# Attention and a SwiGLU block in one kernel: the block's tokens cut into twelve tiles of 512, 512 and 128 instead of nine of 512

## The chip, the core and the metric

The kernel runs on one core of one Trainium2 chip. The metric is the device time of one execution in microseconds (us); of several runs the median is given. A core has five engines with instruction streams of their own: TensorE (PE), VectorE (DVE), ScalarE (ACT), GpSimd (POOL) and SyncE (SP), which here only issues transfers. Each stream is executed in order, and the streams meet at semaphores.

## What is computed

Attention with a forget gate on 8 batches of 8 heads, 576 tokens and 64 columns a head; then the heads' outputs side by side are the 4608 x 512 input of a gated feed-forward block (FFN) with 1536 inner columns.

```python
def _attn_ref(q, k, v, f):
    B, H, S, D = q.shape
    scores = 1.0 / np.sqrt(D) * np.matmul(q, k.transpose(0, 1, 3, 2))
    cum = np.cumsum(np.log(np.clip(f, 0.0001, 1.0)), axis=-1)
    decay = cum[:, :, :, None] - cum[:, :, None, :]
    causal = np.triu(np.ones((S, S), dtype=bool), k=1)
    scores = np.where(causal, -1000000000.0, scores + decay)
    attn = np.exp(scores - np.max(scores, axis=-1, keepdims=True))
    attn = attn / (np.sum(attn, axis=-1, keepdims=True) + 1e-09)
    return np.matmul(attn, v)

def reference(q, k, v, f, moe_w_gate, moe_w_val, moe_w_out):
    x = _attn_ref(q, k, v, f).transpose(0, 2, 1, 3).reshape(4608, 512)
    g = x @ moe_w_gate
    return (g * (1.0 / (1.0 + np.exp(-g))) * (x @ moe_w_val)) @ moe_w_out
```

## The kernel before

**Order.** The program is not written in the order in which it runs. Each piece of work is an `Op` with the engines that may run it, an estimated duration, what it comes after, the buffers it takes and a key. `Plan.run` plays the pieces forward in an estimated time: whenever an engine is free, it takes the ready piece with the lowest key whose buffers are free, and emits its instructions. What comes out is a fixed order on each engine. `ORDER` overrides the keys of the earliest pieces with tuned numbers. `release(p)` gives the estimated time at which a pair of heads may start to load (PACE0, PACE_A and PACE are its offset and its steps; LEAD is how much earlier the conversion of Q and K to bf16 in DRAM is issued on POOL).

**Attention.** Two heads are a pair, four pairs a batch. Scores (`score`, L703) have keys on the partitions and come in four banks of PSUM a head: 7 matmuls, 1600 columns. ACT takes the exponential (`expo`, L737), POOL zeroes the triangle on the diagonal (`mask`, L746), PE weighs the values (`weigh`, L760, 15 matmuls of 65 columns a head, the last column being the sum), DVE inverts the sum and scales (`invert` L767, `scale` L772). The result is transposed into `xT`, a ring for the inputs of six batches (6 x 576 = 3456 columns).

**FFN.** Tokens go in tiles t = 0 to 8 of 512, each cut into 12 chunks (fc) of 128 inner columns. `gate` (L918) makes one chunk's gate or value in one PSUM bank: 4 matmuls of 512 columns, or 8 where a tile wraps round the ring. `tanh` (ACT, L922) and `silu` (DVE, L932) form the activation, `times` (DVE, L935) multiplies it by the value into `HH`. From chunk ALONE on, when all exponentials are done, ACT computes the whole activation with another table (`whole`, L925) and `silu` falls away.

The projection by `w_out` (`wo`) comes in two forms. Tiles t < QUICK use `simple`: 48 matmuls of 512 columns (`project`, L976), copies on ACT (L979), four stores. The others use `finish`, one level of a seven-product scheme in the manner of Strassen over blocks of tokens, inner columns and outputs: `sums` (DVE, L960) prepares three operands for each pair of chunks (512, 512 and 256 columns), `product` (L969) does 2 x 42 matmuls of 256 columns, and ACT (L985), POOL (`both` L992, `apart` L1017) and DVE (`more` L996, `close` L1020) combine the pieces in `OT`. The weights that this needs are made from `wo` by `blend` (DVE, L948 and L950), ten operations of which the last four overwrite `wo` itself, so they come after the last plain projection. The last tile has a finer ending of its own (L1001 to L1013), with stores from SP and ACT.

**Buffers.** PSUM has eight banks: pool f with four (gates and values, also products), s with two (scores), o and t with one each. After the planner's time WIDE_AT the FFN may use all eight. V comes through NNV buffers `natv` by SP's queue (`ld_v`, L612) and is converted on POOL. The transposes of Q and K (`turned`, L599), the gate rows (L602), the transposes of the outputs (`cross`, L790) and most stores also go through SP's queue.

Of the kernel before, what the change touches and what calls it, by code (L numbers as in the profile page):

```python
# [10 lines left out]
BF16 = mybir.dt.bfloat16  # L11
AF = mybir.ActivationFunctionType
ALU = mybir.AluOpType
# [21 lines left out]
class Plan:  # L35
# [163 lines left out]
HALF = 256  # L199
RING = 6  # L200
# [7 lines left out]
OFFS = [0, 0, 576, 1024]  # L208
PT_W = 1408
PADS = (512, 960, 1344)  # L210
NQK, NPT0, NPT, NVB, NNV, NXN, NTH, NHH, NSU, NOT, NRC = 8, 6, 5, 3, 5, 4, 4, 7, 6, 2, 4
FIRST = 2
CROSS = (8, 9, 10)
PACE = 8.6
LATE = 2.5
PACE_A = 9.0
PACE0 = 59.0
LEAD = 14.0


@with_exitstack
def kernel(ctx, tc, q, k, v, f, w_gate, w_val, w_out, out):
    nc = tc.nc
    B, H, S, D = q.shape
    BH = B * H
    N_TOK, DM = out.shape
    DFF = w_gate.shape[1]
    P = 128
# [3 lines left out]
    KD = DM // P  # L232
    KF = DFF // P
    MT = 512
# [5 lines left out]
    FCG, FCO = KF // NCG, KF // NCO  # L240
# [27 lines left out]
    TH = [sb(f"th{i}", [P, MT], F32) for i in range(NTH)]  # L268
    HH = [sb(f"hh{i}", [P, 2, MT], BF16) for i in range(NHH)]
    SU = [sb(f"su{i}", [P, 5, HALF], BF16) for i in range(NSU)]  # L270
    OT = [sb(f"ot{i}", [P, 2, DM], F32) for i in range(NOT)]
    wt = sb("wt", [P, 3, KF // 2, HALF], BF16)
    ident = sb("ident", [P, P], BF16)
# [7 lines left out]
    def ps(b):  # L281
        return bank[bank_of[b.pool] + b.i]
# [12 lines left out]
    QN = [[t.rearrange("p (u x) -> p u x", u=2) for t in ts] for ts in (  # L295
        [SU[r].rearrange("p n c -> p (n c)")[:, : 2 * S] for r in range(KD)], [xT[:, r, 4 * S : 6 * S] for r in range(KD)])]

    plan = Plan(
        {"f": 4, "s": 2, "o": 1, "t": 1, "qk": NQK, "pt0": NPT0, "pt": NPT, "vb": NVB, "nv": NNV,
         "xn": NXN, "rc": NRC, "th": NTH, "hh": NHH, "su": NSU, "ot": NOT},  # L300
        lambda t: 2.0 if t < TWARM else 1.0,
    )
# [165 lines left out]
    def blank(e, what):  # L468
# [46 lines left out]
        else:  # L515
            if what != "rest":
                fill32(e, VB[what][:, :, :, D:].bitcast(F32), ONE2)
            if what:
# [4 lines left out]
              after=[op(("DVE", 0.07), lambda e: nc.vector.memset(warm, 1.0), key=-30)])  # L523
# [23 lines left out]
    for h, name, i in fixed + [(hqk[FB + p], "qk", 2 + p) for p in range(FB)]:  # L547
        h.pool, h.i = name, i
        plan.free[name].remove(i)
    release = lambda p: 0.0 if p < 2 * FB else PACE0 + min(p - 2 * FB, FB) * PACE_A + max(p - 3 * FB, 0) * PACE  # L550

# [240 lines left out]
    x_ready, crossed = {}, {}  # L792
# [30 lines left out]
    exps = []  # L823
# [87 lines left out]
    def gate(e, w, fc, t0, n, bf):  # L911
        lo = t0 % (RING * S)
        cut = min(n, RING * S - lo)
        for ko in range(KD):
            for a, b in ((0, cut), (cut, n)):
                if a < b:
                    at = (lo + a) % (RING * S)
                    nc.tensor.matmul(ps(bf)[:, a:b], w[:, ko, fc * P : (fc + 1) * P], xT[:, ko, at : at + b - a],  # L918
                                     start=ko == 0 and a == 0, stop=ko == KD - 1 and b == n)

    def tanh(e, n, bf, bt):
        nc.scalar.activation(TH[bt.i][:, :n], ps(bf)[:, :n], AF.Tanh, scale=0.5)  # L922

# [10 lines left out]
    def times(e, n, bf, bt, bh, r, lo, by):  # L934
        nc.vector.scalar_tensor_tensor(out=HH[bh.i][:, r, lo : lo + n], in0=TH[bt.i][:, :n], scalar=by, in1=ps(bf)[:, :n],  # L935
                                       op0=ALU.mult, op1=ALU.mult)

    wq = wo.rearrange("p (g e) (s d) -> p e s g d", e=2, s=2)
    B11, B12, B21, B22 = [wq[:, i, j] for i in range(2) for j in range(2)]
    T1, T6, T7 = [wt[:, i] for i in range(3)]  # L940
    T3, T4 = B12, B21
# [10 lines left out]
    def sums(e, n, bh, bu):  # L952
        h, u = HH[bh.i], SU[bu.i]
        if n == 0:
# [17 lines left out]
    def project(e, hs, q, a, bf, gs):  # L972
        lo = a * HALF + q * P
        for g in gs:
            for r in range(2):
                nc.tensor.matmul(ps(bf), HH[hs[g].i][:, r, lo : lo + P], wo[:, 2 * g + r], start=g + r == 0, stop=2 * g + r == KF - 1)  # L976

    def out_copy(e, a, bf, bo):
        nc.scalar.activation(OT[bo.i][:, a], ps(bf), AF.Copy)  # L979

    def store2(e, t0, bo):
        E[e].dma_start(out=bass.AP(out.tensor, out.offset + t0 * DM, [[DM, P], [HALF * DM, 2], [1, DM]]), in_=OT[bo.i])

    def mid_copy(e, bf, bo):
        nc.scalar.activation(OT[bo.i].rearrange("p a d -> p (a d)")[:, HALF : 3 * HALF], ps(bf), AF.Copy)  # L985

    def edges(bo):
        return OT[bo.i].rearrange("p a (s d) -> p (a s) d", s=2)[:, 0::3]

# [35 lines left out]
    w_ready = {}  # L1025
    last_gate = [None]
    tails = []

    before, tabled = [], []

    def unit(t, fc, t0, n, hs, lo, kk, after):
        if (t, fc) == ALONE:
            tabled.append(op(("ACT", 1.4), turn_table, after=before + exps, key=-6, tag="table"))
# [9 lines left out]
        if fresh:  # L1043
            hs[p].gate = g
        alone = (t, fc) >= ALONE
        if alone:
# [13 lines left out]
    read = []  # L1060

    def ffn(t, t0, n):
        key, hs, ms = 1e5 * (t + 1), [None] * (KF // 2), []
        for fc in range(KF):
            parts = [(0, HALF), (HALF, n - HALF)] if t == 0 and fc < WIDE else [(0, n)]
            ms.append([])
            for u, (lo, w) in enumerate(parts):
                lg, m = unit(t, fc, t0 + lo, w, hs, lo, key + 100 * fc + 50 * u, [last_gate[0]])
                ms[fc].append(m)
        last_gate[0] = lg  # L1070
        tails.append((t, t0, key, hs, ms))

    plain = []

# [105 lines left out]
            queries(p, 1000 * b + 100 * (p % FB) + 10)  # L1180
    for p in range(FB, BH // 2):
        attention(p, 1000 * (p // FB) + 1000 + 100 * (p % FB))
    for t, t0 in enumerate(range(0, N_TOK, MT)):
        ffn(t, t0, MT)
    for r in tails[:QUICK]:
        simple(*r)
    ready = [w_ready["o", c] for c in range(NCO)]
    blended = [op({e: f((KF // 2) * HALF // 2) + 0.35 * (n // 2 == 1) for e, f in BLEND_ON.items()}, blend, n, after=ready, key=BLEND_KEY + n, ready=BLEND_AT, tag=("blend", n)) for n in range(6)]
    blended += [op({e: f((KF // 2) * HALF // 2) for e, f in BLEND_ON.items()}, blend, n, after=blended[:6] + plain, key=BLEND_KEY + n, ready=BLEND_AT, tag=("blend", n)) for n in range(6, 10)]
    for r in tails[QUICK:]:  # L1190
        finish(*r, blended)

    for a, b, done in x_ready.values():
        for lo, hi, ops in read:
# [13 lines left out]

QUICK = 3


def F_POOLS(t):
    return ("f",) + tuple((x, WIDE_AT, 1e9) for x in "sot")
# [6 lines left out]
def fast(n):  # L1222
    return (n / 2 + 110) / 960
# [11 lines left out]
BOTH_ON = {"POOL": pool2}  # L1235
APART_ON = {"POOL": pool2}
BLEND_ON = {"DVE": fast}
BLEND_AT = 150.0
POOL_KEY = 50000
ALONE = (6, 6)  # L1240
LAST_ON = {"DVE": slow}
VB1_KEY = 2
QKZ_KEY = -26
# [124 lines left out]
```

## Time and profile before

| | |
|---|---|
| median of 3 runs | 378.27 us (378.03 to 378.41) |
| the profiled execution | 378.08 us |
| its span, first to last instruction | 376.4 us |
| PE busy | 368.8 us, 3427 matmuls |
| DVE busy | 249.4 us, 575 instructions |
| ACT busy | 214.4 us |
| POOL busy | 161.4 us |
| granted PE clock | 1.0 |

Lines of the profile name an engine, the line of the kernel (L918), the tile written and those read, the shape, the count, the busy time and the mean of one in ns, then the idle time of the engine before them and what ended it. "PEld" is the loading of PE's stationary operand, which overlaps PE. A "window" is the busy time of each engine in a stretch of the span. The "chain" follows the work that ended last back through what released it.

### The profile page before, as it was taken

How to read it: one execution, taken by the hardware profiler on the slowest of the kernel's cores; microseconds unless marked ns; L12 is line 12 of the kernel's file. 1: busy time of each engine (PE TensorE's matmuls, PEld its weight loads, DVE VectorE, ACT ScalarE, POOL GpSimd, SP SyncE). 2: the span in 40 equal slices, each digit the busy share in tenths (PEclk: the TensorE clock that was granted, in tenths of full speed). 3: DMA queues.
4: the chain of work that ended last, by engine and by line, in shares of the span. 5: the costliest groups of instructions: out<-in, count | busy, mean ns of one | idle time of the engine just before them, and what ended most of it. 6: DMA issues, size and time to landing. Idle time of an engine off the chain costs nothing.

```text
span 376.4 us, 9092 instructions
## 1 busy us (share of the span) xinstructions
PE 368.8 (98%) x3427; PEld 233.6 (62%) x3427; DVE 249.4 (66%) x575; ACT 214.4 (57%) x438; POOL 161.4 (43%) x388
## 2 busy tenths in 40 slices
PE   8999999999999999999999999999999999999996
PEld 5667655455565555555685558655887776467465
DVE  7979886277526674499737994598638844753664
ACT  7999962265656754746576467555774433333332
POOL 8897546033633643465376437732462013003000
PEclk9999999999999999999999999999999999999999
DMA  8999998859988998999699999995325003002003
GB/s 145 192 198 195 206 204 151 185 100 180 174 187 169 166 189 160 228 191 180 117 160 200 228 149 143 243 206 99 72 74 93 2 2 111 2 0 81 33 0 114
DMA packets 125163, 52.01 MB, mean 138 GB/s; under 512 B 111823, under 2 KB 119695, under 8 KB 124351
## 3 DMA queue, kind: packets, MB, share of 16 engines
q1 hardware_dynamic: 108478, 35.95, 49.2%
q0 software_dynamic: 16288, 15.14, 26.9%
q8 instruction: 27, 0.44, 0.5%
q10 hardware_dynamic: 352, 0.34, 0.3%
q14 instruction: 18, 0.14, 0.1%
HBM read 38.56 MB, written 17.07 MB: 148 GB/s over the span
## 4 chain that ended last, share of the span: by engine, by line
PE 94%; DMA 2%; DVE 1%; POOL 1%; ACT 1%; issue 1%; DVEq 0%; POOLq 0%
PE ps L918 49%; PE ps L969 14%; PE ps L703 10%; PE ps L976 8%; PE ps L760 8%; DMA su<-in_k_dram 2%; PE ps L721 1%; PE ps L777 1%; PE ps L578 1%; POOL su L554 1%; PE ps L729 0%; PE ps L1201 0%; ACT PT L737 0%; DVE hh L935 0%; DVE xn L772 0%
## 5 line engine op out<-in xcount | busy, mean ns | idle before, releaser
L918 PE MATMUL ps<-xT,wv 128*128 128x512 bf16 (+2 forms) x496 | 111.7, 351 | 0.0
L918 PE MATMUL ps<-xT,wg 128*128 128x512 bf16 (+2 forms) x496 | 111.5, 351 | 0.0
L737 ACT ACTIVATE PT<-ps 128x384 bf16<-128x384 f32 (+2 forms) x192 | 91.6, 510 | 14.8 <-PE ps L703 9.7
L935 DVE SCALAR_TENSOR_TENSOR hh<-th,ps 128x512 bf16<-128x512 f32 (+1 forms) x112 | 74.5, 667 | 21.1 <-PE ps L918 12.9
L922 ACT ACTIVATE th<-ps 128x512 f32<-128x512 f32 (+1 forms) x82 | 47.2, 577 | 54.1 <-PE ps L918 51.8
L746 POOL TENSOR_SCALAR_AFFINE_SELECT PT<-PT 128x128 bf16<-128x128 bf16 (+1 forms) x192 | 54.1, 288 | 44.1 <-ACT PT L737 38.5
L918 PEld LDWEIGHTS <-wg 128*128 128x128 bf16 x496 | 45.1, 97 | 37.9
L918 PEld LDWEIGHTS <-wv 128*128 128x128 bf16 x496 | 45.0, 97 | 38.1
L932 DVE SCALAR_TENSOR_TENSOR th<-th,ps 128x512 f32<-128x512 f32 (+1 forms) x82 | 53.7, 656 | 19.7 <-ACT th L922 19.6
L703 PE MATMUL ps<-QK 68*128 68x256 bf16 x392 | 63.9, 261 | 0.4 <-ACT PTa L737 0.4
L746 POOL TENSOR_SCALAR_AFFINE_SELECT PTa<-PTa 128x256 bf16<-128x256 bf16 x64 | 26.3, 413 | 80.3 <-ACT PTa L737 79.5
L760 PE MATMUL ps<-VB,PT 128*128 128x65 bf16 x768 | 42.0, 193 | 0.0
L703 PEld LDWEIGHTS <-QK 68*128 68x128 bf16 x392 | 31.5, 97 | 14.0 <-issue 0.6
L760 PEld LDWEIGHTS <-PT 128*128 128x128 bf16 x768 | 34.2, 97 | 9.3 <-POOL PT L746 0.9
L737 ACT ACTIVATE PTa<-ps 128x384 bf16<-128x384 f32 x64 | 30.9, 488 | 15.4 <-PE ps L703 14.8
L767 DVE RECIPROCAL rc<-ps 128x5 f32<-128x5 f32 (+2 forms) x68 | 12.8, 188 | 39.6 <-PE ps L760 39.3
L969 PEld LDWEIGHTS <-su 128*128 128x128 bf16 x360 | 34.8, 97 | 4.6
L960 DVE TENSOR_TENSOR su<-hh 128x512 bf16<-128x512 bf16 (+1 forms) x108 | 36.7, 384 | 0.9
L925 ACT ACTIVATE th<-ps 128x512 f32<-128x512 f32 x30 | 17.9, 596 | 32.1 <-PE ps L918 32.1
L976 PE MATMUL ps<-wo,hh 128*128 128x512 bf16 x144 | 34.8, 379 | 0.0
L772 DVE TENSOR_TENSOR xn<-ps,rc 128x320 bf16<-128x320 f32 (+2 forms) x72 | 32.4, 454 | 2.2
L969 PE MATMUL ps<-wt,su 128*128 128x256 bf16 x216 | 29.0, 272 | 0.0
(97 smaller groups left out, 323.1 us busy)
## 6 DMA issues: line engine op xcount, KB each, us to landing
out_dram<-ot SPq DMA_DIRECT2D x32, 256.0 KB
natv<-in_v_dram SPq DMA_DIRECT2D x25, 256.0 KB
qk_d<-in_q_dram POOLq DMA_DIRECT2D x24, 144.0 KB, 3.6
qk_d<-in_k_dram POOLq DMA_DIRECT2D x24, 144.0 KB, 4.3
wv<-in_moe_w_val_dram POOLq DMA_DIRECT2D x3, 512.0 KB, 10.6
wg<-in_moe_w_gate_dram POOLq DMA_DIRECT2D x3, 512.0 KB, 12.4
wo<-in_moe_w_out_dram POOLq DMA_DIRECT2D x4, 384.0 KB, 14.1
VB<-in_v_dram POOLq DMA_DIRECT2D x7, 128.0 KB, 8.9
```

The costliest lines, as they stand in the source:

```text
L703: nc.tensor.matmul(s[:, c : c + w], QK[:KR, hqk[p].i, 1, j * S + kt * P : j * S + (kt + 1) * P], QK[:KR, hqk[p].i, 0, j * S + q0 : j * S + ...
L737: nc.scalar.activation(place(h, i)[:, OFFS[i] : OFFS[i] + c], ps(bs)[:, :c], AF.Exp, scale=0.125)
L746: nc.gpsimd.affine_select(out=d, in_=d, pattern=pat, compare_op=ALU.is_ge, fill=0.0, base=0, channel_multiplier=-1,)
L760: nc.tensor.matmul(o[:, lo : lo + D + 1], pt[:, c : c + P], VB[hvb[b].i][:, kt, hb, : D + 1], start=first and n == 0, stop=last and n == l ...
L772: nc.vector.tensor_mul(XN[bx.i][:, qb : qb + nq, j], o, r)
L918: nc.tensor.matmul(ps(bf)[:, a:b], w[:, ko, fc * P : (fc + 1) * P], xT[:, ko, at : at + b - a], start=ko == 0 and a == 0, stop=ko == KD - ...
L922: nc.scalar.activation(TH[bt.i][:, :n], ps(bf)[:, :n], AF.Tanh, scale=0.5)
L932: nc.vector.scalar_tensor_tensor(out=t, in0=t, scalar=1.0, in1=ps(bf)[:, :n], op0=ALU.add, op1=ALU.mult)
L935: nc.vector.scalar_tensor_tensor(out=HH[bh.i][:, r, lo : lo + n], in0=TH[bt.i][:, :n], scalar=by, in1=ps(bf)[:, :n], op0=ALU.mult, op1=ALU ...
L960: E[e].tensor_tensor(out=o, in0=x, in1=y, op=f)
L969: nc.tensor.matmul(ps(bf)[:, c * HALF : (c + 1) * HALF], left(g)[:, q * P : (q + 1) * P], right[:, g], start=opens and g == 0, stop=g == K ...
L976: nc.tensor.matmul(ps(bf), HH[hs[g].i][:, r, lo : lo + P], wo[:, 2 * g + r], start=g + r == 0, stop=2 * g + r == KF - 1)
```

## The change

The tokens are cut into tiles of 512, 512 and 128, four times, so that three tiles are two batches of 576 and no tile wraps round the ring. Tiles of 512 are treated as before, but only tile 0 has the plain projection (QUICK 3 to 1); the other seven have the seven products, so the blends are made earlier (BLEND_AT 150 to 69).

A tile of 128 has functions of its own. `gate4` puts four chunks side by side into one bank, with 16 matmuls of 128 columns; so ACT and DVE still handle 512 columns at a time. `times4` writes the product for four chunks into `NH`, and `pairs` adds neighbouring chunks. `single` projects with H1 B11 + H2 B21 = (H1 + H2) B11 + H2 (B21 - B11), and the same way for the other half of the outputs, since the plain blocks are overwritten by then: 24 matmuls of 256 columns, and in the last tile 12 of 256 and 24 of 128, with three copies and three stores. `lone` orders this.

`natv` goes from 5 to 3 buffers, the loads of the pairs begin somewhat earlier (PACE0, LEAD) with a slightly longer step (PACE), and the activation table is changed at tile 8, chunk 0 instead of tile 6, chunk 6: the same 1280 tokens before the end.

```diff
-NQK, NPT0, NPT, NVB, NNV, NXN, NTH, NHH, NSU, NOT, NRC = 8, 6, 5, 3, 5, 4, 4, 7, 6, 2, 4
+NQK, NPT0, NPT, NVB, NNV, NXN, NTH, NHH, NSU, NOT, NRC = 8, 6, 5, 3, 3, 4, 4, 7, 6, 2, 4
-PACE = 8.6
+PACE = 8.7
-PACE0 = 59.0
-LEAD = 14.0
+PACE0 = 57.0
+LEAD = 16.0
...
+    NH = sb("nh", [P, 3 * KF // 2, P], BF16)
...
+    def gate4(e, w, fq, t0, bf):
+        lo = t0 % (RING * S)
+        for c in range(4):
+            for ko in range(KD):
+                nc.tensor.matmul(ps(bf)[:, c * P : (c + 1) * P], w[:, ko, (4 * fq + c) * P : (4 * fq + c + 1) * P], xT[:, ko, lo : lo + P],
+                                 start=c + ko == 0, stop=c == 3 and ko == KD - 1)
...
+    def times4(e, fq, bf, bt, by):
+        nc.vector.scalar_tensor_tensor(out=NH[:, 4 * fq : 4 * fq + 4].rearrange("p a c -> p (a c)"), in0=TH[bt.i], scalar=by, in1=ps(bf),
+                                       op0=ALU.mult, op1=ALU.mult)
+
+    def pairs(e, fq):
+        h = NH[:, 4 * fq : 4 * fq + 4].rearrange("p (g e) c -> p e g c", e=2)
+        E[e].tensor_tensor(out=NH[:, KF + 2 * fq : KF + 2 * fq + 2], in0=h[:, 0], in1=h[:, 1], op=ALU.add)
...
+    def single(e, s, gs, bf, c0, c1, opens, closes):
+        lo = s * HALF
+        for g in gs:
+            for n, (left, right) in enumerate(((KF + g, B11), (2 * g + 1, T4)) if s == 0 else ((2 * g, T3), (KF + g, B22))):
+                nc.tensor.matmul(ps(bf)[:, c0:c1], NH[:, left], right[:, g, c0 - lo : c1 - lo],
+                                 start=opens and g + n == 0, stop=closes and g + n == KF // 2, skip_group_check=True)
+
+    def part_copy(e, bf, bo, c0, c1):
+        copy(e, OT[bo.i][:, 0, c0:c1], ps(bf)[:, c0:c1])
...
+    def ffn1(t, t0):
+        key, bn, ms, first = 1e5 * (t + 1), Buf("nh"), [], []
+        for fq in range(KF // 4):
...
+            g = op(("PE", mm(*[P] * 4 * KD)), gate4, wg, fq, t0, bg, after=needs + wr + [last_gate[0]], behind=first, take=[bg] + ([] if fq else [bn]), key=kk, tag=("gp", t, 4 * fq))
...
+                b = op(("DVE", dve(MT)), silu, MT, bg, bt, after=[b], use=[bg, bt], key=-5, tag=("silu", t, 4 * fq))
+            a = op(("PE", mm(*[P] * 4 * KD)), gate4, wv, fq, t0, bv, after=[g], take=[bv], key=kk + 1, tag=("vp", t, 4 * fq))
+            m = op(("DVE", dve(MT)), times4, fq, bv, bt, 1.0 if alone else 0.5, after=[a, b] + first, use=[bv, bt, bn], key=-5, tag=("mul", t, 4 * fq))
+            ms.append(op({"DVE": fast(HALF)}, pairs, fq, after=[m], use=[bn], key=-5, tag=("pairs", t, fq)))
...
+    def lone(t, t0, key, bn, ms, blended):
+        bo, end, taken = Buf("ot"), t0 + P == N_TOK, False
+        cuts, last, bf = ((0, HALF), (HALF, HALF + P), (HALF + P, DM)) if end else ((0, HALF), (HALF, DM)), [], None
+        for n, (c0, c1) in enumerate(cuts):
...
+            for fq in range(KF // 4):
+                gs = (2 * fq, 2 * fq + 1)
+                last = [op(("PE", mm(*[c1 - c0] * 4)), single, c0 // HALF, gs, bf, c0, c1, opens, closes, after=blended + [ms[fq]] + last,
+                           take=[bf] if opens and not fq else [], use=[bn] + ([] if opens and not fq else [bf]), key=key + 2000 + 100 * n + fq + (150, 51, 0)[n] * (end and fq > 1), tag=("fo", t, n, fq))]
+            if closes:
...
+                c = op(("DVE", dve(c1 - lo)) if end and n else ("ACT", act(c1 - lo)), part_copy, bf, bo, lo, c1, after=last, take=[] if n and end else [bo], use=[bf] + ([bo] if n and end else []),
+                       key=-4, tag=("ot", t, n))
+                op(("ACT" if end and n == 1 else "SP", 0.45 if end else 0.7), store, t0, 0, bo, slice(lo, c1), after=[c], use=[bo], key=-4, dma=0.5 if end else 1.0, packet=90, tag=("out", t, n))
...
-    for t, t0 in enumerate(range(0, N_TOK, MT)):
-        ffn(t, t0, MT)
+    t0 = 0
+    for t, n in enumerate(TILES):
+        ffn(t, t0, n) if n == MT else ffn1(t, t0)
+        t0 += n
...
-        finish(*r, blended)
+        (finish if TILES[r[0]] == MT else lone)(*r, blended)
...
-QUICK = 3
+QUICK = 1
+TILES = (512, 512, 128) * 3 + (512, 512, 128)
...
-BLEND_AT = 150.0
+BLEND_AT = 69.0
-ALONE = (6, 6)
+ALONE = (8, 0)
```

More of the change, by code (lines that the diff above doesn't have):

```diff
@@ L299 @@
         {"f": 4, "s": 2, "o": 1, "t": 1, "qk": NQK, "pt0": NPT0, "pt": NPT, "vb": NVB, "nv": NNV,
-         "xn": NXN, "rc": NRC, "th": NTH, "hh": NHH, "su": NSU, "ot": NOT},
+         "xn": NXN, "rc": NRC, "th": NTH, "hh": NHH, "nh": 1, "su": NSU, "ot": NOT},
         lambda t: 2.0 if t < TWARM else 1.0,
@@ L1071, in ffn @@
         tails.append((t, t0, key, hs, ms))
+    def ffn1(t, t0):
+        key, bn, ms, first = 1e5 * (t + 1), Buf("nh"), [], []
+        for fq in range(KF // 4):
+            if (t, 4 * fq) == ALONE:
+                tabled.append(op(("ACT", 1.4), turn_table, after=before + exps, key=-6, tag="table"))
+            needs = [o for a, b, done in x_ready.values() if a < t0 + P and b > t0 for o in done]
+            wr = [w_ready[n, c] for n in "gv" for c in range(4 * fq // FCG, (4 * fq + 3) // FCG + 1)]
+            bg, bv, bt = Buf(*F_POOLS(t)), Buf(*F_POOLS(t)), Buf("th")
+            kk = key + 400 * fq
+            g = op(("PE", mm(*[P] * 4 * KD)), gate4, wg, fq, t0, bg, after=needs + wr + [last_gate[0]], behind=first, take=[bg] + ([] if fq else [bn]), key=kk, tag=("gp", t, 4 * fq))
+            first = first or [g]
+            alone = (t, 4 * fq) >= ALONE
+            if alone:
+                b = op(("ACT", act(MT)), whole, MT, bg, bt, after=[g] + tabled, take=[bt], use=[bg], key=-5, tag=("tanh", t, 4 * fq))
+            else:
+                b = op(("ACT", act(MT)), tanh, MT, bg, bt, after=[g], take=[bt], use=[bg], key=-5, tag=("tanh", t, 4 * fq))
+                before.append(b)
+                b = op(("DVE", dve(MT)), silu, MT, bg, bt, after=[b], use=[bg, bt], key=-5, tag=("silu", t, 4 * fq))
+            a = op(("PE", mm(*[P] * 4 * KD)), gate4, wv, fq, t0, bv, after=[g], take=[bv], key=kk + 1, tag=("vp", t, 4 * fq))
+            m = op(("DVE", dve(MT)), times4, fq, bv, bt, 1.0 if alone else 0.5, after=[a, b] + first, use=[bv, bt, bn], key=-5, tag=("mul", t, 4 * fq))
+            ms.append(op({"DVE": fast(HALF)}, pairs, fq, after=[m], use=[bn], key=-5, tag=("pairs", t, fq)))
+            read.append((t0, t0 + P, [g, a]))
+        last_gate[0] = g
+        tails.append((t, t0, key, bn, ms))
@@ new lines, in lone @@
+    def lone(t, t0, key, bn, ms, blended):
+        bo, end, taken = Buf("ot"), t0 + P == N_TOK, False
+        cuts, last, bf = ((0, HALF), (HALF, HALF + P), (HALF + P, DM)) if end else ((0, HALF), (HALF, DM)), [], None
+        for n, (c0, c1) in enumerate(cuts):
+            opens = bf is None or end
+            if opens:
+                bf, last = Buf(*F_POOLS(t)), []
+            closes = end or c1 == DM
+            for fq in range(KF // 4):
[3 more added lines that the diff above has]
+            if closes:
+                lo = c0 if end else 0
+                c = op(("DVE", dve(c1 - lo)) if end and n else ("ACT", act(c1 - lo)), part_copy, bf, bo, lo, c1, after=last, take=[] if n and end else [bo], use=[bf] + ([bo] if n and end else []),
+                       key=-4, tag=("ot", t, n))
+                op(("ACT" if end and n == 1 else "SP", 0.45 if end else 0.7), store, t0, 0, bo, slice(lo, c1), after=[c], use=[bo], key=-4, dma=0.5 if end else 1.0, packet=90, tag=("out", t, n))
```

## The prediction, made before the changed kernel ran

> **What bounds the kernel now.** I read the page's busy table and slices first, then the windows of 20 us, then who waits on PE, and last the chain in order of time with the groups by shape.
>
> ```profile
> span 376.4 us, 9092 instructions
> ...
> PE 368.8 (98%) x3427; PEld 233.6 (62%) x3427; DVE 249.4 (66%) x575; ACT 214.4 (57%) x438; POOL 161.4 (43%) x388
> ...
> PE   8999999999999999999999999999999999999996
> ```
>
> PE is busy in every slice but the first and the last, so the time is PE's stream of matmuls, plus its gaps, plus what follows the last matmul. Small gaps do not show in that digit, since a matmul's modelled end overlaps the next one. The chain gives the spacing:
>
> ```profile
> 66.08 0.46 PE ps L760 x15
> ...
> 286.25 19.19 PE ps L918 x168
> 305.44 9.17 PE ps L969 x84
> 314.61 20.72 PE ps L918 x96
> ```
>
> 84 products of 256 columns in 9.17 us are 109.2 ns each; 96 gate matmuls of 512 columns in 20.72 us are 215.8 ns each. The difference is 106.6 ns for 256 columns, 0.4164 ns a column, which leaves 2.6 ns for each matmul whatever its width. The 168 are 8 of 512 and 80 pairs of 384 and 128 (the tile that wraps round the ring): (19.19 - 1.73)/80 = 218.3 ns a pair, 2.5 ns more than one of 512. So a split costs the fixed part and nothing else. The second engine is DVE:
>
> ```profile
> 60.00:80.00 20.00, 20.00 (x147) 10.43 (x146) 8.69 (x19) 5.83 (x11) 3.79 (x9) 1.00 0.93 172
> ...
> 160.00:180.00 20.00, 19.44 (x147) 10.26 (x146) 19.06 (x40) 10.81 (x23) 11.51 (x25) 1.00 1.09 182
> 180.00:200.00 20.00, 19.49 (x219) 15.32 (x217) 10.40 (x27) 14.01 (x31) 12.56 (x31) 1.00 0.90 159
> 200.00:220.00 20.00, 19.87 (x143) 10.35 (x141) 18.40 (x38) 10.36 (x22) 8.57 (x21) 1.00 1.08 187
> ```
>
> (The stretch, PE, PEld, DVE, ACT and POOL busy.) From 160 to 180 us, the gates of the first tile with seven products, DVE has 19.06 of 20 us, and just there and after it PE loses 0.56, 0.51 and 0.13 us. The page's waits of PE name it:
>
> ```profile
> PE ps L1201 <- DVE warm L523: 1.1, 1, 1.1
> PE ps L760 <- DVE xn L772: 0.6, 1, 0.6
> PE ps L562 <- DMA su<-in_k_dram: 0.5, 2, 0.4
> ```
>
> The first and the third are the start; no later wait of PE in that view names a DMA.
>
> **The change part by part.** Counts are of the two programs in their order; durations from the rows.
>
> *Matmuls.* Up to tile one's first two gates (about 75 us) PE's order is the same. After that, two tiles' plain projections go: 3 x 48 matmuls of 512 become 48. Products of 256 go from 504 to 588 (seven tiles instead of six), the four narrow tiles project with 108 matmuls in 24576 columns, and their gates are 384 matmuls of 128. Tiles and batches now fit the ring, so the 96 splits of the wrapped tile vanish. In all 861760 columns become 858688, and 3427 matmuls become 3715. That is -3072 x 0.4164 = -1.28 us and +288 x 2.6 ns = +0.75 us: **-0.53 us**. No row of before has a long run of 128-column gate matmuls, each with its own weight load; I bound the fixed part by 2.5 ns (the split pairs) below, and above by the load not hiding, which is a rival below. I take 2.6, because a 65-column matmul with a full load of its own comes every 0.46/15 = 31 ns, well under the 56 ns of a 128-column one.
>
> The Trainium skill's page "TensorE: Matmul & The Clock Gate", section "Back-to-back issue gap", says that in a real stream of load and multiply pairs a matmul of 128 columns takes about 81 ns instead of 56. By it the 384 narrow gates would cost some 9.6 us more (an estimate from that page) and the change would lose. The same passage gives 131 ns for 512 columns, where this trace has 215.8; the trace decides.
>
> *DVE.* Per group:
>
> ```profile
> L935 DVE SCALAR_TENSOR_TENSOR hh<-th,ps 128x512 bf16<-128x512 f32 x104 | 71.3, 686 | 20.7 <-PE ps L918 12.9 <-PE ps L703 0.6
> L932 DVE SCALAR_TENSOR_TENSOR th<-th,ps 128x512 f32<-128x512 f32 x74 | 50.4, 681 | 18.8 <-ACT th L922 18.8
> L960 DVE TENSOR_TENSOR su<-hh 128x512 bf16<-128x512 bf16 x72 | 28.4, 427 | 0.9
> L772 DVE TENSOR_TENSOR xn<-ps,rc 128x320 bf16<-128x320 f32 x56 | 27.5, 491 | 1.8
> L960 DVE TENSOR_TENSOR su<-hh 128x256 bf16<-128x256 bf16 x36 | 10.8, 299 | 0.0
> L767 DVE RECIPROCAL rc<-ps 128x5 f32<-128x5 f32 x56 | 10.7, 191 | 38.0 <-PE ps L760 37.8
> L1020 DVE TENSOR_TENSOR ot<-ps,ot 128x512 f32<-128x512 f32 x11 | 7.6, 690 | 16.0 <-POOL ot L1017 14.9 <-PE ps L703 0.9
> L996 DVE TENSOR_TENSOR ot<-ps,ot 128x256 f32<-128x256 f32 x12 | 5.1, 425 | 13.4 <-POOL ot L992 5.3 <-PE ps L969 4.1 <-POOL PTa L746 2.1
> ...
> L948 DVE TENSOR_TENSOR wt<-wo 128x768 bf16<-128x768 bf16 x6 | 3.1, 551 | 0.0
> ...
> L948 DVE TENSOR_TENSOR wo<-wo 128x768 bf16<-128x768 bf16 x4 | 2.5, 662 | 0.0
> ```
>
> One more tile with sums adds 12 x 0.427 + 6 x 0.299 = 6.9 us, its closing 2 x (0.425 + 0.690) = 2.2, the twelve `pairs` at 0.299 (same size as the narrow sum) 3.6: 12.7 us, DVE 249 to 262. The average is harmless; what counts is DVE against PE between a tile's first and last value gate. Before, tile 3 has 12 `times`, 11 `silu`, 9 wide and 4 narrow sums, 6 blends (2 and 4) and 5 heads' norms (0.682 each): 27.9 us, against 88 gates, 28 scores and 75 weighings on PE, 24.0 us: 3.9 too much. Tile 4: 24.9 against 23.5, 1.4 too much. What that cost shows from the first gate to the first product:
>
> ```profile
> 155.29 1.03 PE L918 MATMUL ps<-xT,wg 128*128 128x512 bf16 x4
> ...
> 183.63 0.82 PE L969 MATMUL ps<-wo,hh 128*128 128x256 bf16 x6
> ...
> 198.41 0.81 PE L918 MATMUL ps<-xT,wg 128*128 128x512 bf16 x3
> ...
> 225.34 0.82 PE L969 MATMUL ps<-wo,hh 128*128 128x256 bf16 x6
> ```
>
> Tile 3 took 28.34 us for 213 matmuls with 62737 columns, 26.68 us at the spacing above: 1.66 lost. Tile 4: 26.93 for 26.20, 0.73 lost. About half of the excess each time; the four banks of pool f take up the rest. After the change the blends go into tile 1 (BLEND_AT 69: four stand before its first `silu`, six among its gates). Tile 1: 28.0 against 24.9, 3.1 too much; tile 3: 24.2 against 23.9; tile 4: 24.9 against 24.0; tile 6: 24.9 against 24.3. Half of these: 1.5 + 0.15 + 0.45 + 0.3 = 2.4, against 1.66 + 0.73 + nothing for tile 5 (25.6 against 25.8) = 2.4 before. With the blends that still stand in front of tile 1 nothing is sure here: from -1.7 (tile 1's backlog swallowed by the slack that the 8.69 of 20 us at 60 to 80 shows) to +1.6 (all of its 3.1 lost). I take **-0.1**, since the first four blends, 2.2 us, fall into that slack.
>
> *The end.*
>
> ```profile
> 371.84 0.82 PE L969 MATMUL ps<-wt,su 128*128 128x256 bf16 x6
> ...
> 372.46 0.42 DVE L1009 SCALAR_TENSOR_TENSOR ot<-ps,ot 128x256 f32<-128x256 f32 x1
> 372.99 0.42 DVE L1013 TENSOR_TENSOR ot<-ps,ot 128x256 f32<-128x256 f32 x1
> ```
>
> PE ends at 372.66, the last closing at 373.41 behind another closing on DVE, and the span 2.95 us later with the store. After, the last thing is a copy of 128 columns: 0.425 - (0.690 - 0.425)/2 = 0.29 us, with nothing queued ahead of it: 0.1 + 0.29 + 2.95 = 3.35 instead of 3.70. In front of it, the last narrow group needs `times4` (0.69), `pairs` (0.30) and two handovers of some 0.15, 1.3 us, while PE has 8 narrow matmuls of 256 and 8 of 128 columns, 1.32 us. On DVE these also queue behind tile ten's last closing, which waits for POOL:
>
> ```profile
> L985 ACT ACTIVATE ot<-ps 128x512 f32<-128x512 f32 x22 | 13.1, 597 | 20.1 <-PE ps L969 19.9
> L1017 POOL TENSOR_TENSOR ot<-ot 128x512 f32<-128x512 f32 x10 | 12.7, 1266 | 11.3 <-ACT ot L985 11.3
> ```
>
> 0.60 + 1.27 + 0.69 and three handovers are some 3 us after that tile's m2, and PE has 0.66 us of products and 3.6 us of narrow gates there; it just fits. I charge 0.1: **-0.25 us**, bounds -0.4 and +0.3.
>
> *Costed at nothing.* Three natv buffers instead of five: SP's V loads now wait for POOL's casts, and the transposes of Q and K queue behind them on SP. The cover is the lead, which grows by 2 us, and that PE waited for no DMA after the start; without it, each wait on a late transpose reaches the next scores. PACE, PACE0 and LEAD move loads by at most 2 us at both ends. The table load moves with ALONE to the same 1280 tokens from the end. POOL's 4 us more of `both` and `apart` lie in stages in which it has 8.6 to 12.6 of 20 us. Stores go out under the next tile's gates.
>
> Sum: -0.53 - 0.1 - 0.25 = -0.9 us of span. The profiled execution took 378.08 us with its 376.4 of span; less 0.9 is 377.2. The median is 0.19 above that execution, so **377.3 us** is what I compare with 378.27.
>
> **Rivals.**
> - *A tie.* The backlog costs as much more as the end saves, or a late transpose eats 0.5 us: -0.53 + 0.1 or so, 377.8. For it: all three terms are small.
> - *DVE becomes the bound in the gates.* Place: tiles 1, 3, 4 and 6, all with sums now and all during attention; before, only two of its tiles were over. Price: if each loses what tile 3 lost, 4 x 1.66 = 6.6 instead of 2.4, so +4.2 - 0.8 = +3.4: 381.7. It decides once DVE's work passes PE's by more than some 2 us in a gate stage, where the banks no longer take it up; tile 1 passes it, the others by count do not. With only tile 1 at its full 3.1 (+1.6) the time is 379.1.
> - *The narrow weight loads do not hide.* The load of a gate tile lasts 97 ns by its row; if it set the spacing, 384 x (97 - 56) = 15.7 us more, 393. It decides once a load takes longer than the matmul before it and cannot start earlier. Against it stand the 31 ns. (The rule weighed above, of "TensorE: Matmul & The Clock Gate" in the Trainium skill, is this one.)
>
> ```profile
> L918 PEld LDWEIGHTS <-wg 128*128 128x128 bf16 x496 | 45.1, 97 | 37.9
> ```
>
> - *The backlog goes away* with the blends out of the busy stage: -1.7 instead of -0.1, 378.27 - 0.53 - 1.7 - 0.25 = 375.8.
> - *That it does not do what it says* can be left out: the order has 588 products and 384 narrow gates.
>
> **How the numbers follow.** Forecast 0.53 (376.5 to 377.6), tie 0.20, DVE 0.19, narrow loads 0.02, backlog gone 0.06. What a measurement here tells from no change is about 0.2%, 0.76 us, so faster means under 377.5. The forecast's own range reaches to that line, so a little of it is in the tie: faster 0.57, same 0.22, slower 0.21. The range reaches from the backlog's gain, 375.8, to a tile 1 that loses everything and a little of the others, 379.6.
>
> **What would show it.** Runs of sixteen narrow gates taking 0.89 us in the chain (1.3 would be the loads); products 84 in 9.17 as before. Tile 1's gates to its first product: 27.85 us of matmuls; up to 29.5 is the forecast, 31 the DVE rival. No loss at 160 to 220 us beyond half a microsecond. From the last matmul to the end 3.3 to 3.4 us. I would be wrong by a wait of PE on a DMA or on `pairs`, or by tiles 3, 4 and 6 losing over 0.7 us each.

## The result, and the profile after

| | before | after |
|---|---|---|
| median of 7 runs each | 378.31 us (378.03 to 378.84) | 379.36 us (379.29 to 380.35) |
| ratio after / before | | 1.0035, 95% interval 1.0024 to 1.0047 |
| the profiled execution | 378.08 us | 379.88 us |

The changed kernel is slower by 0.35%; 377.3 us was forecast. Its page, as before the span, the busy times and PE's row of the slices:

```profile
span 378.1 us, 9696 instructions
...
PE 369.3 (98%) x3715; PEld 248.7 (66%) x3715; DVE 259.9 (69%) x605; ACT 213.3 (56%) x436; POOL 168.6 (45%) x396
...
PE   8899999999999999999999999999999999999996
```

PE is as full as before at this resolution. To see the gaps, I took each matmul's start in the trace and subtracted the sum of the spacings of all matmuls ahead of it (2.55 ns and 0.4167 ns a column). What is left grows only where PE stands still. With what follows the last matmul, the span then has four parts:

| us | before | after | change | forecast |
|---|---|---|---|---|
| matmuls at their spacing | 367.81 | 367.26 | -0.55 | -0.53 |
| gaps up to tile 1's first gate | 1.18 | 1.70 | +0.52 | none |
| gaps from there on | 3.51 | 6.04 | +2.53 | -0.1 |
| after the last matmul's spacing | 3.86 | 3.08 | -0.78 | -0.25 |

The second row is left aside: this one execution lies 0.52 us above its kernel's median, and in the profiles of the experiments below the start loses anything from 0.8 to 3.3 us. The third row is the result. By stage:

| us lost by PE | after | forecast |
|---|---|---|
| tile 1, first gate to first product (73.2 to 102.6 us) | 1.51 | 1.5 |
| tile 1, its products (to 116.2) | 1.23 | none |
| tile 3, first gate to first product | 0.97 | 0.15 |
| tile 3, its products | 0.52 | none |
| tile 4, first gate to first product | 0.94 | 0.45 |
| tile 6, first gate to first product | 0.44 | 0.3 |
| all else | 0.43 | none |

The windows of after (the stretch; then PE, PEld, DVE, ACT and POOL busy):

```profile
60.00:80.00 20.00, 20.00 (x150) 10.34 (x147) 12.23 (x27) 4.86 (x10) 3.68 (x8) 1.00 0.98 196
80.00:100.00 20.00, 19.05 (x159) 10.66 (x157) 19.17 (x40) 12.81 (x29) 11.08 (x27) 1.00 0.86 155
100.00:120.00 20.00, 19.34 (x256) 16.46 (x254) 12.41 (x28) 12.07 (x26) 13.59 (x32) 1.00 0.78 127
140.00:160.00 20.00, 19.56 (x191) 12.69 (x188) 15.19 (x35) 12.77 (x27) 9.40 (x27) 1.00 0.94 153
```

The full stretch of DVE has moved from 160 to 80 us and is as full as it was there, 19.17 of 20 us. PE loses in it, but also in the next one and at 140 to 160 us, where DVE has only 12.41 and 15.19. So DVE's volume alone doesn't place the losses. The waits say what does (who waits, for whom, us in total, times, the longest):

```profile
POOL VB L330 <- DMA natv<-in_v_dram: 6.6, 3, 4.8
...
PE ps L761 <- DVE xn L773: 1.7, 4, 0.8
...
PE ps L1272 <- DVE warm L524: 1.1, 1, 1.1
...
PE ps L733 <- issue: 1.0, 1, 1.0
...
PE ps L985 <- DVE hh L943: 0.2, 1, 0.2
...
PE ps L985 <- DVE su L976: 0.2, 1, 0.2
```

L761, L773, L943, L976 and L985 are `weigh`, `scale`, `times`, `sums` and `product`, which were L760, L772, L935, L960 and L969. No row of the view has a gate of PE waiting, so it is not the four banks of pool f. PE waits in attention above all: `weigh` of a head for `scale` of the head before. The longest of these waits in the timeline (start, duration, engine, line, operation; idle time before it and its releaser in brackets):

```profile
94.30 0.84 DVE L976 TENSOR_TENSOR su<-hh 128x512 bf16<-128x512 bf16 x2
...
94.50 0.52 PE L761 MATMUL ps<-VB,PT 128*128 128x65 bf16 x12
...
95.06 0.67 DVE L940 SCALAR_TENSOR_TENSOR th<-th,ps 128x512 f32<-128x512 f32 x1
...
95.84 0.69 DVE L943 SCALAR_TENSOR_TENSOR hh<-th,ps 128x512 bf16<-128x512 f32 x1
95.86 0.55 PE L704 MATMUL ps<-QK 68*128 68x256 bf16 x4
...
96.45 0.19 DVE L768 RECIPROCAL rc<-ps 128x5 f32<-128x5 f32 x1
...
96.67 0.49 DVE L773 TENSOR_TENSOR xn<-ps,rc 128x320 bf16<-128x320 f32 x1
...
97.21 0.25 PE L761 MATMUL ps<-VB,PTa 128*128 128x65 bf16 x3 [0.81 <-DVE xn L773]
```

One head's weighing ends at 95.02. Its `invert` could start then, but DVE still works off two sums, a `silu` and a `times`, and gets to it at 96.45. Until `scale` ends at 97.16 the head's outputs stand in the one bank of pool o, and the next head's weighing can't open it. PE, which runs in order, stands still with gates queued behind that weighing.

Added up over all steps of more than 0.06 us from tile 1's first gate on, and by what ended each, PE's waits for `scale` are 3.35 us (1.13 before), those for `times` and sums 0.70 (none before), those for ACT's exponentials and POOL's masks 0.93 (1.29 before). Smaller steps make 1.06 (1.10 before). So `scale` accounts for 2.2 of the 2.53 us.

Of the 1.23 us in tile 1's products, 1.15 are three waits in a row, for a `times`, a sum and a `scale` (0.37, 0.33 and 0.45 us by the spacing). Ahead of all three on DVE stands one sum that took 2.23 us:

```profile
100.57 2.23 DVE L976 TENSOR_TENSOR su<-hh 128x512 bf16<-128x512 bf16 x1
102.11 0.40 POOL L747 TENSOR_SCALAR_AFFINE_SELECT PTa<-PTa 128x256 bf16<-128x256 bf16 x1
...
104.26 0.28 PE L985 MATMUL ps<-wo,hh 128*128 128x256 bf16 x1 [0.21 <-DVE hh L943]
...
105.25 0.94 PE L985 MATMUL ps<-wt,su 128*128 128x256 bf16 x7 [0.17 <-DVE su L976]
...
106.48 0.25 PE L761 MATMUL ps<-VB,PTa 128*128 128x65 bf16 x3 [0.28 <-DVE xn L773]
```

During that sum POOL worked without a pause, on two casts of V and then on masks. Of the 84 sums of this size in the trace, the 52 that ran while POOL stood still took 0.42 us, none over 0.43; the 32 that met an instruction of POOL took 0.56 on average. In all the other runs' traces, too, no such sum over 0.43 us is without POOL beside it. That POOL's work causes it is likely, but no run separates the two.

### The profile page after: what moved, and what is told of

Same layout as the page of the kernel before. It is cut to its first block, busy times and chain, and to the rows that moved or that the text cites. A ratio compares the mean times of both kernels' runs of the same rounds, so it can differ in the third digit from the quotient of the medians.

```text
span 378.1 us, 9696 instructions
## 1 busy us (share of the span) xinstructions
PE 369.3 (98%) x3715; PEld 248.7 (66%) x3715; DVE 259.9 (69%) x605; ACT 213.3 (56%) x436; POOL 168.6 (45%) x396
## 4 chain that ended last, share of the span: by engine, by line
PE 87%; DVE 6%; DMA 2%; ACT 2%; issue 1%; POOL 0%; DVEq 0%; ACTq 0%; POOLq 0%
PE ps L919 40%; PE ps L985 16%; PE ps L704 9%; PE ps L761 8%; PE ps L926 5%; PE ps L998 3%; PE ps L992 3%; DVE hh L943 2%; DVE su L976 2%; DMA su<-in_q_dram 1%; DVE th L940 1%; DMA natv<-in_v_dram 1%; DVE xn L773 1%; PE ps L722 1%; PE ps L778 1%
## 5 line engine op out<-in xcount | busy, mean ns | idle before, releaser
L919 PE MATMUL ps<-xT,wv 128*128 128x512 bf16 (+1 forms) x400 | 99.3, 370 | 0.0
L919 PE MATMUL ps<-xT,wg 128*128 128x512 bf16 (+1 forms) x400 | 99.1, 370 | 0.0
L943 DVE SCALAR_TENSOR_TENSOR hh<-th,ps 128x512 bf16<-128x512 f32 (+1 forms) x100 | 66.2, 664 | 23.3 <-PE ps L919 16.3
L704 PE MATMUL ps<-QK 68*128 68x256 bf16 x392 | 63.0, 261 | 0.0
L919 PEld LDWEIGHTS <-wg 128*128 128x128 bf16 x400 | 37.7, 97 | 34.5
L919 PEld LDWEIGHTS <-wv 128*128 128x128 bf16 x400 | 37.5, 97 | 34.5
L976 DVE TENSOR_TENSOR su<-hh 128x512 bf16<-128x512 bf16 (+1 forms) x126 | 46.6, 413 | 1.1
L985 PEld LDWEIGHTS <-su 128*128 128x128 bf16 x420 | 40.1, 98 | 5.5 <-DVE su L976 0.4
L761 PE MATMUL ps<-VB,PT 128*128 128x65 bf16 x768 | 41.9, 193 | 0.0
L761 PEld LDWEIGHTS <-PT 128*128 128x128 bf16 x768 | 34.7, 97 | 7.5 <-POOL PT L747 0.6
L1018 POOL TENSOR_TENSOR ot<-ot 128x256 f32<-128x256 f32 x14 | 10.1, 722 | 63.7 <-ACT ot L1011 63.7
L773 DVE TENSOR_TENSOR xn<-ps,rc 128x320 bf16<-128x320 f32 (+2 forms) x72 | 32.4, 453 | 2.2
L985 PE MATMUL ps<-wt,su 128*128 128x256 bf16 x252 | 33.2, 272 | 0.2 <-DVE su L976 0.2
```

Of the source, the lines that this page charges most:

```text
L704: nc.tensor.matmul(s[:, c : c + w], QK[:KR, hqk[p].i, 1, j * S + kt * P : j * S + (kt + 1) * P], QK[:KR, hqk[p].i, 0, j * S + q0 : j * S + ...
L761: nc.tensor.matmul(o[:, lo : lo + D + 1], pt[:, c : c + P], VB[hvb[b].i][:, kt, hb, : D + 1], start=first and n == 0, stop=last and n == l ...
L773: nc.vector.tensor_mul(XN[bx.i][:, qb : qb + nq, j], o, r)
L976: E[e].tensor_tensor(out=o, in0=x, in1=y, op=f)
L985: nc.tensor.matmul(ps(bf)[:, c * HALF : (c + 1) * HALF], left(g)[:, q * P : (q + 1) * P], right[:, g], start=opens and g == 0, stop=g == K ...
```

## The experiments

Each ran in five rounds beside the kernel before on the same chip, whose median was 378.6 us each time; ratios are to that. The changed kernel itself was not measured there: its 379.36 us stands beside 378.31. Differences to it are given by the medians; by the ratios they come out 0.2 to 0.8 us larger (for e3, 3.6 us instead of 2.8). The table shows where PE lost time, by the sums above, from one profile each. Single numbers are good to some 0.3 us, since these profiles lack up to 1% of the matmul records.

| us lost | start | tile 1 | tiles 2, 3 | rest | all | median, us |
|---|---|---|---|---|---|---|
| after | 1.7 | 2.7 | 1.5 | 1.8 | 7.7 | 379.36 |
| e1 tile 1 plain | 2.5 | 0.4 | 1.2 | 2.1 | 6.2 | 378.79 |
| e3 second bank | 1.4 | 0.9 | 1.1 | 1.1 | 4.5 | 376.58 |
| e5 blends earlier | 1.4 | 0.2 | 1.5 | 2.2 | 5.3 | 377.54 |
| e6 old pace | 1.3 | 0.6 | 1.0 | 2.6 | 5.5 | 378.10 |
| e7 second bank, durations | 0.8 | 0.9 | 0.9 | 1.0 | 3.5 | 376.47 |
| e8 second bank, blends earlier | 1.4 | 0.1 | 0.8 | 1.1 | 3.4 | 376.09 |
| e9 second bank, old pace | 1.2 | 1.8 | 0.9 | 1.3 | 5.2 | 377.39 |
| e10 blends earlier, old pace | 1.3 | 1.4 | 1.0 | 3.0 | 6.7 | 379.31 |
| e11 second bank, blends, old pace | 3.3 | 0.3 | 0.8 | 1.0 | 5.5 | 376.77 |
| e12 second bank, blends, durations | 1.2 | 0.3 | 0.8 | 0.9 | 3.2 | 375.36 |

**Tile 1 without sums.** Tile 1 gets the plain projection again, and nothing else changes.

```diff
-QUICK = 1
+QUICK = 2
```

> The changed kernel with tile 1 projected plainly as well (QUICK 2), everything else kept. Theory (DVE backlog): the sums of tile 1 leave its gate stage, so most of the 2.6 us that PE lost between tile 1's first gate and the end of its products goes; 3072 columns come back (+1.28 us) with 36 matmuls fewer (-0.09). About 378.5 us, PE losing under 0.6 us from 73 to 107 us of the span. Rival one (narrow gates or their weight loads cost it): nothing but the columns changes, 380.5. Rival two (the new pace of the loads): the same 380.5.

378.79 us (some 378.5 expected), ratio 1.0006 (0.9988 to 1.0023). Tile 1's loss falls from 2.7 to 0.4. The window of e1:

```profile
80.00:100.00 20.00, 19.84 (x173) 11.40 (x174) 14.28 (x27) 13.70 (x29) 9.95 (x28) 1.00 0.84 158
```

With 14.28 instead of 19.17 us of DVE the stage is nearly clean. Its profile spent 0.8 us more at the start than that of after, and the later stages lose as they did: the rest of the loss isn't tile 1's.

**The kernel before with its sums as early.** Only the sums move; the tiles stay nine of 512.

```diff
-QUICK = 3
+QUICK = 1
...
-BLEND_AT = 150.0
+BLEND_AT = 69.0
```

> The kernel before, nine tiles of 512 and its own pace, with only QUICK 1 and BLEND_AT 69: seven products in tiles 1 and 2 too. By the matmuls alone -6144 columns and +72 matmuls, -2.4 us: 375.9, which is what the rivals (narrow tiles, pace) expect. Theory (DVE backlog): tile 1 loses some 2.6 us as in the changed kernel and tile 2 some 1 us, tile 3 gets back about 0.8 of its 1.7 without the blends: 378.5 to 379.5, with DVE over 19 of 20 us at 80 to 100.

385.08 us, ratio 1.0175 (1.0131 to 1.0219), worse than every forecast. The gaps are 13.6 us; tile 1 loses 2.3 of them, near the forecast, but tile 2 loses 2.3 as well. Its waits of PE and two links of its chain:

```profile
PE ps L760 <- DVE xn L772: 2.4, 5, 1.1
PE ps L703 <- DMA QK<-dec_d: 1.2, 1, 1.2
...
PE ps L760 <- POOL VB L329: 0.7, 1, 0.7
PE ps L703 <- ACT PT L737: 0.7, 3, 0.2
```

```profile
121.29 4.08 SPq L599
125.47 4.71 DMA QK<-dec_d
```

The wait for `scale` leads again, so the narrow tiles don't bring it. Here, though, scores also wait for gate rows that stood behind transposes on SP's queue (1.4 us by the spacing, at 130 us). And from 156 to 164 us PE has heads and no gates to put between them: nine times, 2.7 us together by the spacing, its scores wait for ACT's exponentials. So this run shows the wait without narrow tiles, but its 385 us are not DVE's alone.

**A second bank for the heads.** The bank of pool t may take a head's weighing from the planner's 75 us on. Volumes stay the same on every engine.

```diff
-            bo, ws, x1 = Buf("o"), [], None
+            bo, ws, x1 = Buf("o", ("t", 75.0, 1e9)), [], None
```

> The changed kernel, with the idle bank of pool t as a second one for attention's output from 75 us of the planner's time on, so that the first weighing of a head needn't wait until DVE has scaled the head before. Theory (the backlog reaches PE through that single bank): the waits of PE on the scaling, 1.7 us in the view of waits and some 3 us in the spacing, shrink by more than half: 376.5 to 377.7. Rival (the backlog reaches PE through the gate banks of pool f, or the order of the sums): no more than 0.4 us gained, 379 or above.

376.58 us, ratio 0.994 (0.992 to 0.9959): the loss turns into a gain. PE's waits and the window and timeline of e3 at the place shown above:

```profile
PE ps L1272 <- DVE warm L524: 1.1, 1, 1.1
PE ps L733 <- issue: 0.8, 1, 0.8
PE ps L563 <- ACT QK L328: 0.7, 1, 0.7
PE ps L985 <- DVE hh L943: 0.4, 1, 0.4
```

```profile
80.00:100.00 20.00, 19.84 (x174) 11.61 (x176) 19.17 (x41) 13.92 (x30) 12.96 (x30) 1.00 0.84 155
```

```profile
93.91 0.52 PE L761 MATMUL ps<-VB,PT 128*128 128x65 bf16 x12
...
94.41 0.25 PE L761 MATMUL ps<-VB,PTa 128*128 128x65 bf16 x3
...
96.51 0.49 DVE L773 TENSOR_TENSOR xn<-ps,rc 128x320 bf16<-128x320 f32 x1
```

DVE is exactly as full, 19.17 of 20 us, and as late: the head weighed by 94.43 is scaled at 96.51. But the next head's weighing starts at 94.41, 2.1 us ahead of that scaling. The waits for `scale` are gone from the view, and tile 1 loses 0.9 instead of 2.7. Over the whole kernel, counted by steps as above, they fall from 3.35 to 0.12 us, and all gaps from tile 1's first gate on from 6.0 to 3.0. One reservation: the planner's order moves with the second bank, and e3's longest sum takes 0.87 us instead of 2.23, so up to 0.5 us of this, the difference in tile 1's products, may not be the bank's.

**The same bank for the kernel before.**

> The kernel before with the same second bank for attention's output. Theory: its tiles 3 and 4 lost 1.66 and 0.73 us, mostly in front of a head's first weighing; more than half of that comes back: 376.5 to 377.3. Rival: unchanged, 378.3.

378.60 us, ratio 1.0001 (0.9984 to 1.0018), a miss: I had forecast a gain. From tile 3's first gate to its first product the loss falls from 1.65 to 1.03 us, but in its products it grows from 0.18 to 0.97. In e4's view of waits `scale` is still there, and a sum now holds up a product:

```profile
PE ps L760 <- DVE xn L772: 0.3, 1, 0.3
...
PE ps L969 <- DVE su L960: 0.2, 1, 0.2
```

By the spacing these two waits are 0.52 and 0.33 us, both among tile 3's products: the bank lets PE run ahead, and it meets DVE's backlog there. The other part could not come back: of the 1.03 us before the first product 0.52 are a wait for ACT's exponential and 0.32 one for POOL's mask, and both are as large in the trace of before. In all, this kernel's waits for `scale` were only 1.13 us; 0.80 are left.

**Blends earlier.** Still with one bank; now all blends but the last stand ahead of tile 1's products of gate and value.

```diff
-BLEND_AT = 69.0
+BLEND_AT = 50.0
```

> The changed kernel with the blends allowed 19 us earlier (BLEND_AT 50), so that eight of the ten stand on DVE before tile 1's first activation instead of four; all else kept. Theory: tile 1's gate stage asks 3 us less of DVE, its excess of 3.1 us goes to about zero, and of the 2.75 us that PE loses from 80 to 120 us some 1.5 or more come back: 377.4 to 378.1. Rival (the sums' place in DVE's order, not the blends): 379.0 or more.

377.54 us, ratio 0.9975 (0.9965 to 0.9986). Counted as in the prediction, tile 1's excess falls from 3.1 to 0.7 us, and its loss from 2.7 to 0.2; the later tiles keep theirs, with waits for `scale` of

```profile
PE ps L761 <- DVE xn L773: 1.3, 4, 0.5
```

in e5's view. So the slack at 60 to 80 us was there, as the prediction hoped; the change didn't use it for the last six blends.

**The old pace.** The three constants of the loads go back.

```diff
-PACE = 8.7
+PACE = 8.6
...
-PACE0 = 57.0
-LEAD = 16.0
+PACE0 = 59.0
+LEAD = 14.0
```

> The changed kernel with the loads' pace of before (PACE 8.6, PACE0 59, LEAD 14). Theory: DVE's work in each tile's gates is the same, so the time stays within 0.5 us of 379.4, though heads may fall at other places in it. Rival (the pace is what made it slower): 378.0 or less.

378.10 us, ratio 0.9981 (0.997 to 0.9992), a miss by 1.3 us and only 0.1 above the rival's line. With the old pace the rest of the change is not slower than the kernel before, but 0.2% faster. Tile 1's excess is 2.8 us, hardly less than in after, yet it loses 0.6 instead of 2.7: the heads fall elsewhere in DVE's order, so PE waits there for no `scale`, and no sum takes more than 0.83 us. Tile 6 now loses 1.1 us in its gates (0.4 in after).

**Blends earlier and the old pace.** Both of these gains together:

> The changed kernel with the blends 19 us earlier and the pace of before, a single bank. Theory: both empty the same loss at 80 to 120 us (2.75 us before, 0.2 with the blends earlier, 0.65 with the old pace), so they don't add: 377.2 to 378.0. If they are two losses, 376.3 or less.

379.31 us, ratio 1.0018 (1.0009 to 1.0026), a miss again: two edits that each gained 1.3 to 1.8 us against after gain nothing together by the medians, and 0.6 us by the ratios. The wait for `scale` is larger than in after, in e10's view,

```profile
PE ps L761 <- DVE xn L773: 2.1, 5, 0.7
```

although DVE is less full than in e3 or after:

```profile
80.00:100.00 20.00, 19.08 (x172) 11.14 (x174) 17.71 (x39) 13.59 (x29) 10.69 (x27) 1.00 0.75 144
```

Tile 1 has an excess of 0.5 us here and loses 1.4; five heads' norms fall among its gates instead of four. With one bank it is the place of each `scale` in DVE's order that costs, and not the volume alone.

**Second bank with each of these.**

> The changed kernel with the second bank for attention's output and the blends 19 us earlier. Theory (two parts of one backlog): with two banks alone 376.6 with 1.0 us lost from 80 to 120 us; without the blends in tile 1 that goes: 375.6 to 376.0. If the two only repair the same loss: 376.5.

> The changed kernel with the second bank and the pace of before. The old pace alone took 1.3 us off, although it left tile 1's excess at 2.8 us. Theory: the pace acts through where a head's first weighing falls behind DVE's queue, so with two banks it has nothing left to act on: within 0.4 us of the 376.6 with two banks alone. Rival (the pace has a cost of its own, in the loads): another 1 us off, 375.5 or less.

> Second bank, blends 19 us earlier, old pace. Theory: nothing left for the pace; within 0.4 us of the 376.1 without it. Tile 4's gates have two more heads and an excess of 2.2 us by count, so rather above than below.

376.09 us, 0.9931 (0.9914 to 0.9948); 377.39 us, 0.9977 (0.9963 to 0.999); 376.77 us, 0.9948 (0.9932 to 0.9963). The first is 0.1 us above its forecast; the other two miss theirs, lying 0.8 and 0.7 us above the runs that they were to equal. With two banks and the blends earlier, tile 1's loss is gone for either pace (0.1 and 0.3). The old pace alone costs 0.8 us on top of e3, where it gained 1.3 with one bank: it shuffles which operations meet, and has no fixed worth. What PE meets in tile 1 of e9 is no longer `scale` but POOL's masks (0.58 and 0.20 us by the spacing) and a wait for gate rows (0.28). Tile 6's 1.1 us under the old pace with one bank are 0.1 with two.

**The planner's durations of DVE.** `silu` and `times` of 512 columns get the 0.69 us that the rows show, and the sums theirs, by a formula that blends and `pairs` share; the planner's order then follows.

```diff
-            b = op(("DVE", dve(n)), silu, n, bg, bt, after=[b], use=[bg, bt], key=-5, tag=("silu", t, fc))
+            b = op(("DVE", 0.16 + n / 976), silu, n, bg, bt, after=[b], use=[bg, bt], key=-5, tag=("silu", t, fc))
...
-    return (n / 2 + 110) / 960
+    return 0.172 + n / 2000
```

> The changed kernel with the second bank for attention's output, and with the planner's estimates of silu, times and the sums on DVE set to the durations of the trace (0.685, 0.43 and 0.30 us instead of 0.61, 0.38 and 0.25), so that it orders PE by what DVE really takes. Theory: the 1.8 us that the run with two banks alone still lost from 100 to 160 us shrink to about 1: 375.6 to 376.2. Rival (the order is as good as can be, DVE's volume is the limit): 376.6 or more.

> Second bank, blends 19 us earlier, and the planner's DVE estimates as measured. By count no tile's gates exceed PE by more than 0.6 us. Theory: at most the 0.8 us still lost from 140 to 160 us to gain, 375.5 to 376.1. If the estimates only reshuffle, 376.1 to 376.6, as two banks with measured estimates (376.5) were no better than two banks alone (376.6).

e7, on e3's version: 376.47 us, 0.994 (0.9924 to 0.9956), no better than e3 and short of its forecast. e12, on e8's version: 375.36 us, 0.9915 (0.9901 to 0.9929), 0.1 us better than forecast. That is the best version found, and it beats both kernels: the one before by 3.2 us (378.57 beside it), the changed one by some 4.5 us, as the ratios 0.9915 and 1.0035 give it. How much of it the durations bring is not shown, as its interval overlaps e8's. PE's waits in e12's view name `scale` no more, with DVE busy for 262.0 us:

```profile
PE ps L1272 <- DVE warm L524: 1.1, 1, 1.1
PE ps L733 <- issue: 0.7, 1, 0.7
PE ps L563 <- DMA su<-in_k_dram: 0.3, 1, 0.3
```

## Why the prediction was wrong

**The step that failed** is the term for DVE: "About half of the excess each time; the four banks of pool f take up the rest", and the -0.1 us drawn from it. It measured +2.5 us. Of that, 2.2 us are waits for `scale`, behind one bank that the sum did not contain. In tile 1, 1.23 us more were lost in the products, which the rule left out: 0.70 there are waits for a `times` and a sum, so DVE's backlog was not taken up either. Tiles 3, 4 and 6, forecast at 0.9 us together, lost 2.35 up to their first products, though their excesses are small; for tiles 3 and 4 the sign of being wrong that the prediction had named, over 0.7 us each, came true.

The rule's number for tile 1 held up to the line at which it was counted (1.51 us lost by the first product, 1.5 forecast), but that was luck. The 1.66 us from which the half was taken contain 0.52 us of waiting for ACT and 0.32 for POOL, between tile 3's last gate and its first product. Two rows of the view of waits of before, which the prediction did not weigh, are these:

```profile
PE ps L703 <- ACT PTa L737: 0.4, 1, 0.4
...
PE ps L760 <- POOL PTa L746: 0.2, 1, 0.2
```

DVE cost that stage 0.72 us, by its one wait for `scale`, a fifth of the excess and not half. And tile 1's volume was undercounted: 28.0 us of DVE between its first and last `times` by the rows' means, 30.2 in the trace of after. The one sum of 2.23 us makes 1.8 of the difference.

The reason is the wrong cushion. The prediction counted volumes, and took the four banks of the gates as what lies between DVE and PE. The row that named the other one was quoted there (PE's 0.6 us for `scale`, L772) and read as a symptom. `scale` empties the only bank of pool o, and on DVE it stands in order behind whatever sums, blends and gate work came first; PE feels each of those meetings at once, even in a stage whose volume fits. e3 shows it: the same work on every engine, a second bank, and 2.8 us come back. e10 shows it from the other side: with a smaller volume in tile 1 its waits for `scale` add up to 3.36 us, as many as in after.

**The rivals.** "DVE becomes the bound in the gates" was the right one, in its lighter form: "With only tile 1 at its full 3.1", 379.1 us. Tile 1 lost 2.7 us, but the path was the single bank and one slow sum rather than the gates' banks, and 379.36 comes so near because the other tiles' extra loss and the better end partly cancel. Its point of decision, an excess of some 2 us, was wrong: e6 has 2.8 and loses 0.6 in tile 1, e10 has 0.5 and loses 1.4. "The backlog goes away" with the blends in the slack is what e5 does to tile 1; the change itself left six among the gates.

**The matmuls** were right: -0.55 for -0.53 us. Narrow gates take what their columns cost, in the chain of after:

```profile
101.86 0.89 PE ps L926 x16
102.75 0.66 PE ps L985 x6
...
301.15 3.57 PE ps L926 x64
```

3.57 us for 64 is 55.8 ns each, and sixteen take 0.89 us as forecast, so the loads hide and the rival of 393 us falls. The Trainium skill's page "TensorE: Matmul & The Clock Gate", section "Back-to-back issue gap", gives about 81 ns for such pairs; this trace does not agree.

**The end** gained more than forecast, -0.78 for -0.25 us. The tail in the timeline of after:

```profile
372.32 2.85 PE L998 MATMUL ps<-wo,nh 128*128 128x256 bf16 x36
...
375.20 0.29 DVE L330 COPY ot<-ps 128x128 f32<-128x128 f32 x1 [0.38 <-PE ps L998]
```

The last 36 matmuls run through almost without a gap, so the 0.1 us charged for a stall in front fell away; the copy is the 0.29 us forecast; and from its end at 375.49 the store takes 2.6 us to the end of the span, where I had kept the 2.95 us of before.

**Costed at nothing** held for SP and the three V buffers as far as the trace shows: POOL waits 6.6 us for V (the row above), but 5.9 of them end by 69 us, where PE's gaps do not grow (1.69 us at 60, 1.71 at 80), and after the start no wait of PE names a DMA. NNV was not tried alone. For the pace of the loads it did not hold: PACE, PACE0 and LEAD were counted only as a shift of 2 us, and e6 shows that, with one bank, they decide on which side of the kernel before the change falls.

## What to carry to other kernels

Sums of an engine's work over a stage aren't enough: find the buffer with a single copy that the late engine empties, and see what queues behind its refill on the bound engine. A second copy there can be worth more than a shift of work (2.8 us here, 1.8 for the blends), but only what the copy itself cost can come back: in e4, where DVE's volume was 3.9 us too much, part of the wait moved on to the products and the rest belonged to other engines. Before a rule is drawn from a measured loss, ask of each wait in it which engine ended it. And with a single copy, retuning by one constant measures how operations happen to meet, so its gain does not add to the next one's.

## What was not expected

One bank more was worth 2.8 us in one kernel and nothing in the other, although both showed the wait for `scale` (3.35 and 1.13 us). A sum on DVE that takes 0.42 us with POOL idle took 2.23 us beside a busy POOL. Loads shifted by 2 us moved the time by 1.3 us down with one bank, and by 0.8 us up with two. And the store of the last 128 columns lands 2.6 us after its copy, against 2.95 us for the store that ended the kernel before.
